# Keys and queries loaded as rows of two positions on 96 partitions instead of eight on 72

## The chip, the cores and the metric

The kernel runs on one core of a Trainium2 chip. Its time is the device time of one execution in microseconds, the median over several runs.

## The reference

Three layers in a row, all in float32:

```python
# attention: q, k, v of 4 batches, 8 heads, 576 positions, 64 dimensions
scores = scale * np.matmul(q, k.transpose(0, 1, 3, 2))
mask = (rel >= 0) & (rel < 64)               # rel = query position - key position
scores = np.where(mask, scores, -1000000000.0)
attn = np.exp(scores - np.max(scores, axis=-1, keepdims=True))
attn = attn / (np.sum(attn, axis=-1, keepdims=True) + 1e-09)
x = np.matmul(attn, v)                       # then 2304 tokens of 512
# one expert of eight for each token, by the largest of xn @ en.T / tau
h = np.maximum(x[mask] @ w1[e], 0.0)
out[mask] = gate_w[mask, None] * (h @ w2[e])
# a layer for all tokens
r = np.maximum(x @ w_in, 0.0)
out = (s * (r * r) + b) @ w_out
```

## The kernel before

The work has three stages: attention with the choice of experts (up to about 200 us), the experts one after the other, and the last layers. The change lies in attention.

Attention works on 16 units, a unit being two heads (hp and hp + 4) of one batch, which lie on the two halves of the partitions. A unit has nine windows of 64 queries; a step takes three windows, so there are 48 steps. In a step TensorE multiplies the queries of a window of both heads (qbd, a block-diagonal tile) with 128 keys (kT) into sp (L250). VectorE adds the mask and takes the minimum (sm and mn, L255), GpSimd takes it off (L258), ScalarE exponentiates into pe (L265, L268), TensorE flips pe into pt (L274), ScalarE copies that to pT (L276), TensorE multiplies pT with the values vb into pob (L285), and VectorE divides into xs (L288 to L290). The PSUM tile pt has one buffer. Between the steps stand transposes of xs (tpx, copied to xt by ScalarE at L382) and the router's products and sums (rt). Most of a step's later operations run one or two steps behind its scores.

Keys and queries arrive with positions on partitions and have to be turned so that the 64 dimensions lie on partitions. load_qk (L159 to L165) loads the keys and the queries of a unit each with one DMA: partition p of 72 gets eight positions in a row, of both heads, 2 KB a head. prep (L217 to L242) turns a unit in four pieces (keys and queries, of two heads each). A piece is four transposes of [72, 128], each of two neighbouring positions (L227), into one PSUM tile tp of three buffers. The upper half of the partitions then holds the even positions, the lower half the odd ones, and two copies bring them to their places in kT or qbd:

```python
o = kT[rows].rearrange("r (p j e) -> r e j p", j=hj, e=2)[:, par]
i = pt[64 * par:64 * par + 64]
```

Neighbouring elements of i thus go to places eight elements (32 bytes) apart. Both copies of the keys, and the even one of the queries, are ScalarE's (L237); the odd one of the queries is VectorE's (L239).

TensorE's order and SyncE's order are the order of the code (manual_schedule). A rule (AHEAD, RATE) spreads the pieces of prep over the steps. The order on ScalarE, VectorE and GpSimd is made by a scheduler that estimates times. After the pieces of unit n stand, on SyncE's queue, the load of unit n + 2's keys and queries, which reuse the four raw buffers, and of unit n + 1's values (L193); between them stand the stores of xs to x_dram (L687). The tau that VectorE turns into itau (L353) comes on ScalarE's DMA queue.

Of the kernel before, what the change touches and what calls it, by code (L numbers as in the profile page):

```python
# [8 lines left out]
F32 = mybir.dt.float32  # L9
# [11 lines left out]
def tile_kernel(ctx, tc, q, k, v, emb, tau, w1, w2, w_in, w_out, s_in, b_in, out, x_dram, y_dram, y0_dram, wi_dram, wo_dram):  # L21
    nc = tc.nc
    B, H, S, D = q.shape
    NT, DM = out.shape
    NP = H // 2
    NW = S // 64
    QP = 72
    QJ = S // QP
    BIG = 3.0e38

    E, _, F = w1.shape
    NTT = NT // 128
    # columns of tokens for the experts, the first one fixed before the others, these by falling count;
    # the first one's first NA columns are fixed early: of TF tiles of tokens, some expert has as many
    TF = 13
    TL = 15
    NA = 208
# [10 lines left out]
    ident = const.tile([128, 128], F32, name="ident")  # L48
    make_identity(nc, ident)

    # token and gate of an expert's columns; the token of a column among all
# [3 lines left out]
    # by order of work: expert, first column  # L55
# [4 lines left out]
    # tiles that are left over: expert, first rank, first column, number  # L60
# [5 lines left out]
    # of a token: its expert (E less it), its rank there; its number and gate in parts  # L66
    km = const.tile([128, NTT], F32, name="km")
    rank = const.tile([128, NTT], F32, name="rank")
# [20 lines left out]
    def load_part(src, le=nc.vector):  # L89
        """a source of [128, 1024], then its high and low parts"""  # L90
        n = nchunk[0]
        nchunk[0] += 1
        ring = rings[0] if n % KR < 8 else rings[1]
        raw = raw_p.tile([128, 1024], F32, tag="raw", name="raw")
        nc.sync.dma_start(raw if len(src.shape) == 2 else raw.rearrange("p (r d) -> p r d", r=2), src)
        h = ring.tile([128, 1024], F32R, tag="wh", name="wh")
        l = ring.tile([128, 1040 if ring is wa else 1024], F32R, tag="wl", name="wl")[:, :1024]
        return (h, l), lambda: split(raw, h, l, le)
# [14 lines left out]
    def turn(pp, xg, xt, o, c0=0):  # L113
        """a tile of rows, transposed, as high and low parts: columns c0.. to o.."""
        r = xg.shape[0]
        tp = pp.tile([128, ND, 128], F32, tag="tp", name="tp")
        for c in range(ND):
            nc.tensor.transpose(tp[:, c, :r], xg[:, c * 128:(c + 1) * 128], ident[:r, :r])
        o1 = o + r - c0
        return split(tp[:, :, c0:r], xt[0][:, :, o:o1], xt[1][:, :, o:o1], nc.vector)  # L120

    def three(ps, a, b, first, last):
        """ps += a[0] b[0] + a[0] b[1] + a[1] b[0], of high and low parts"""
        for j, (x, y) in enumerate(((0, 0), (0, 1), (1, 0))):
            nc.tensor.matmul(ps, a[x], b[y], start=first and j == 0, stop=last and j == 2)  # L125

    def summed(ps, pairs):
        """the like over pairs of a and b, with the low parts of b last"""
        k = [(a[x], b[y]) for x, y in ((0, 0), (1, 0), (0, 1)) for a, b in pairs]
        for j, (x, y) in enumerate(k):  # L130
            nc.tensor.matmul(ps, x, y, start=j == 0, stop=j == len(k) - 1)  # L131
# [27 lines left out]
    def load_qk(b, hp):  # L159
        r = []  # L160
        for nm, src in (("k", k), ("q", q)):
            t = raw_p.tile([128, 1024], F32, tag="raw", name=nm)[:QP].rearrange("p (h d) -> p h d", h=2)
            nc.sync.dma_start(t, src[b].rearrange("(t f) (p j) d -> f p t (j d)", f=NP, p=QP)[hp])
            r.append(t)
        qk[b, hp] = r  # L165
# [5 lines left out]
    # of eight pairs of heads; keys and values in the place of the first weights  # L171
# [16 lines left out]
    def load_v(b, hp):  # L188
        # slots 0..3: blocks 2t | 2t+1 on the halves; 4..7: blocks 2t+1 | 2t+2
        for i in range(2):  # L190
            for h in range(2):
                src = v[b, hp + h * NP, 64 * i:64 * i + 512].rearrange("(w p) d -> p w d", p=128)
                nc.sync.dma_start(vbufs[(b * NP + hp) % NB][:, 4 * i:4 * i + 4, h, :D], src)  # L193
# [7 lines left out]
    # masks: [0] the window of keys i-1, i; [1] the first window, keys 0, 1  # L201
# [15 lines left out]
    def prep(b, hp):  # L217
        """transposes of a pair of heads, in four pieces"""
        kt, qt = qk.pop((b, hp))
        qd = qbd[(b * NP + hp) % NB]  # L220
        kT = kTs[(b * NP + hp) % NB]
        hj = QJ // 2
        for nm, src in (("k", kt), ("q", qt)):
            for h in range(2):
                pt = ps3.tile([128, hj, QP], F32, tag="tp", name="tp")
                for jj in range(hj):
                    nc.tensor.transpose(pt[:, jj], src[:, h, jj * 2 * D:(jj + 1) * 2 * D], ident[:QP, :QP])  # L227
                rows = slice(64 * h, 64 * h + 64)
                for par in range(2):
                    if nm == "k":  # L230
                        o = kT[rows].rearrange("r (p j e) -> r e j p", j=hj, e=2)[:, par]
                        i = pt[64 * par:64 * par + 64]
                    else:
                        o = qd[rows, :, h].rearrange("r w (p j e) -> r e j w p", j=hj, e=2)[:, par]
                        i = pt[64 * par:64 * par + 64].rearrange("r j (w p) -> r j w p", w=NW)
                    if par == 0 or (nm, h) in TOACT:
                        nc.scalar.activation(o, i, AF.Copy)  # L237
                    else:
                        nc.vector.tensor_copy(o, i)  # L239
                if nm == "q" and h == 1:  # L240
                    ready[b, hp] = qd, kT
                yield  # L242
# [91 lines left out]
    def router_setup():  # L334
# [20 lines left out]
        # everything in this bank adds up from zeros  # L355
# [53 lines left out]
    def block(kk, ln, a):  # L409
        """a = 128 kk + ln"""  # L410
        nc.vector.tensor_scalar(kk, a, 1.0 / 128.0, -127.0 / 256.0, op0=ALU.mult, op1=ALU.add)
        nc.vector.tensor_scalar(kk, kk, 12582912.0, -12582912.0, op0=ALU.add, op1=ALU.add)
        nc.vector.scalar_tensor_tensor(ln, kk, -128.0, a, op0=ALU.mult, op1=ALU.add)
# [22 lines left out]
    def route_list(t0, t1):  # L436
        n = t1 - t0
        ts_ = slice(t0, t1)
        # rank among the tokens of the same expert
# [3 lines left out]
        # its tile and its lane there  # L443
# [4 lines left out]
        # the experts' lists of tokens  # L448
# [24 lines left out]
    def route_gate(t0, t1):  # L473
        n = t1 - t0
        ts_ = slice(t0, t1)
        # gate: 1 / (sum exp(l - max) + 1e-9), as three bfloat16 parts that add up to it
# [19 lines left out]
    def route_first(t):  # L496
        """the expert with the most of the first t tiles' tokens"""
        u = rp.tile([128, E], F32, name="uf")
        nc.vector.scalar_tensor_tensor(u, R[:, t], W8, c7, op0=ALU.mult, op1=ALU.add)
        m = rp.tile([128, 1], F32, name="mf")  # L500
        nc.vector.tensor_reduce(m, u, axis=AX.X, op=ALU.max)
        nc.vector.tensor_scalar(ohf, u, m, None, op0=ALU.is_equal)
        ef = rp.tile([1, E], F32, name="ef")
        nc.vector.tensor_tensor(ef, ohf[0:1], iota[0:1, :E], op=ALU.mult)
        ff = rp.tile([1, 1], F32, name="ff")
        nc.vector.tensor_reduce(ff, ef, axis=AX.X, op=ALU.add)
        nc.vector.tensor_copy(efi, ff)
# [8 lines left out]
    def first_list(j0, j1, v0, v1):  # L516
        """values of columns j0..j1 of the first expert's list"""
# [18 lines left out]
    def route_order():  # L536
# [13 lines left out]
        # first column of an expert  # L550
# [13 lines left out]
    def by_order(dst, src, og):  # L564
        """an expert's list, by order of work"""
# [22 lines left out]
    def route_rest(cnt, og, oc):  # L588
        # the token of each column
# [32 lines left out]
        # tiles that the experts' columns don't hold, by expert  # L622
# [36 lines left out]
        # its first rank: the expert's columns and 128 for each tile before, or its last 128 tokens  # L659
# [127 lines left out]
    def first_part():  # L787
        """the first expert's first tokens, in twelve pieces"""
# [48 lines left out]
    # pieces of transposes by step: so many ahead of need, or a rate that stays below RATE  # L837
    AHEAD, RATE = 3, 1.9
    # in steps P0.. to PS the maximum is taken off on GpSimd, one step earlier than the exponentials need it
    P0, PS = 2, 42  # L840
    # pieces of the first expert's first tokens between the last steps
# [70 lines left out]
    def fetch(g):  # L912
        """an expert's tokens"""
# [9 lines left out]
    # between them, the choice of experts for the last tokens, and the rest of that expert's tokens  # L923
    with tc.manual_schedule(engines={mybir.EngineType.PE}):
# [20 lines left out]
        # columns from NA on  # L945
# [57 lines left out]
    def f64_part(n, rp=None):  # L1003
        """32 blocks of [128, 512] of the two weights, from float64 bits to float32, one half before the other"""
# [11 lines left out]
        # the high word's sign, exponent and 20 bits, as a float32  # L1016
        nc.vector.tensor_scalar(t, hi, 3, 0x3fffffff, op0=ALU.logical_shift_left, op1=ALU.bitwise_and)
        nc.vector.scalar_tensor_tensor(t, hi, -(1 << 30), t, op0=ALU.bitwise_and, op1=ALU.bitwise_or)
        # the low word's 32 bits, times that sign and exponent
# [9 lines left out]
    def overflow(mo):  # L1029
        """the tiles of tokens that an expert's own columns don't hold, one at a time"""  # L1030
# [262 lines left out]
```

## Time and profile before

| | |
|---|---|
| median of 3 runs | 855.96 us (855.43 to 857.25) |
| span of the profiled execution | 855.3 us |
| busy share of the span | PE 94%, PEld 87%, DVE 62%, ACT 49%, POOL 29% |
| mean granted TensorE clock | 0.978 |
| DMA packets | 88705, 117.14 MB |

The profile gives the span of the execution from its first to its last instruction and no other time for it. PE is TensorE's matmuls, PEld its weight loads, DVE VectorE, ACT ScalarE, POOL GpSimd, SP SyncE; a q behind the name is the engine's queue. A matmul in float32 shows as two records, a transpose as one. The last column of a timeline row is the idle time of the engine ahead of it and what ended it.

### The profile page before, as it was taken

Reading aid. Unit: us, or ns where it says so; the run is one execution under the profiler, and the core shown is the slowest. Engines: PE = TensorE matmul, PEld = TensorE weight load, DVE = VectorE, ACT = ScalarE, POOL = GpSimd, SP = SyncE. Lnnn points to the kernel's source line nnn. Section 1 sums busy time; section 2 is a strip of 40 time slices with the busy share of each in tenths; the row PEclk is TensorE's granted clock in tenths of the full one; section 3 lists DMA queues with packets and bytes.
Section 4 is the critical chain, followed back from the end, with each engine's and each line's share of the span. In section 5 each row is a group of like instructions: output and inputs, shape, how many; then the busy total and the mean of one; then the engine's idle time right before and its main releaser. Section 6 shows DMA issues by size and latency. Waiting matters only on the chain. (4 is left out here: it accounts for less than half of the span.)

```text
span 855.3 us, 16295 instructions
## 1 busy us (share of the span) xinstructions
PE 806.6 (94%) x6142; PEld 743.9 (87%) x6142; DVE 532.3 (62%) x1358; ACT 415.5 (49%) x813; POOL 251.1 (29%) x281
## 2 busy tenths in 40 slices
PE   5989988689999999989899999999999999999997
PEld 4868777579999999979899999999999999998885
DVE  4567798777787786879765555566655444444442
ACT  6798786541534545445354444444545333233331
POOL 6156764543201514524402222222210110111110
PEclk9799999889999999999989999999999999999999
DMA  8787763715666877788275222233332211100000
GB/s 178 150 194 147 156 130 74 225 33 180 216 198 233 285 246 237 250 268 287 105 246 175 86 97 99 99 117 112 114 114 79 72 50 50 50 26 25 25 25 25
DMA packets 88705, 117.14 MB, mean 137 GB/s; under 512 B 38468, under 2 KB 57924, under 8 KB 88624
## 3 DMA queue, kind: packets, MB, share of 16 engines
q1 hardware_dynamic: 79136, 99.11, 39.7%
q0 software_dynamic: 3232, 10.24, 3.3%
q10 hardware_dynamic: 6256, 6.72, 2.4%
q8 instruction: 49, 0.80, 0.4%
q14 instruction: 32, 0.26, 0.1%
HBM read 91.52 MB, written 24.53 MB: 136 GB/s over the span
## 5 line engine op out<-in xcount | busy, mean ns | idle before, releaser
L125 PE MATMUL p<-xl,wh 128*128 128x256 f32 x576 | 162.4, 282 | 0.0
L125 PE MATMUL p<-xh,wh 128*128 128x256 f32 x576 | 162.2, 282 | 0.0
L125 PE MATMUL p<-xh,wl 128*128 128x256 f32 x576 | 161.7, 281 | 0.0
L1200 ACT ACTIVATE r<-p 128x256 f32<-128x256 f32 x144 | 55.3, 384 | 167.8 <-PE p L125 164.7
L1201 DVE SCALAR_TENSOR_TENSOR r<-r,s_bc 128x256 f32<-128x256 f32 x144 | 80.9, 564 | 81.4 <-ACT r L1200 81.3
L1024 POOL TENSOR_TENSOR fl<-fl,fs 128x512 f32<-128x512 f32 x32 | 45.8, 1433 | 251.6 <-DVE fs L1023 226.7
L125 PE MATMUL p<-wh,gh 128*128 128x512 f32 x288 | 113.0, 392 | 0.0
L125 PE MATMUL p<-wl,gh 128*128 128x512 f32 x288 | 113.0, 392 | 0.0
L125 PE MATMUL p<-wh,gl 128*128 128x512 f32 x288 | 113.0, 392 | 0.0
L125 PEld LDWEIGHTS p<-xh,wh 128*128 128x128 f32 x576 | 108.8, 189 | 0.7
L125 PEld LDWEIGHTS p<-xl,wh 128*128 128x128 f32 x576 | 108.6, 189 | 0.8
L125 PEld LDWEIGHTS p<-xh,wl 128*128 128x128 f32 x576 | 109.0, 189 | 0.0
L87 DVE TENSOR_TENSOR wl<-raw,wh 128x1024 fp32r<-128x1024 f32 x72 | 101.9, 1423 | 7.0 <-ACT wh L86 6.7
L86 ACT ACTIVATE wh<-raw 128x1024 fp32r<-128x1024 f32 x80 | 83.2, 1056 | 6.6 <-DMA raw<-wo_dram 3.4
L125 PE MATMUL p<-hh,wh 128*128 128x256 f32 (+5 forms) x256 | 78.7, 307 | 0.0
L1239 POOL DMA_INDIRECT out_dram<-o,ids x18 | 19.1, 1061 | 202.9 <-DVE o L1238 181.5
L125 PE MATMUL p<-hl,wh 128*128 128x256 f32 (+5 forms) x256 | 77.0, 301 | 0.0
L125 PE MATMUL p<-hh,wl 128*128 128x256 f32 (+5 forms) x256 | 76.9, 300 | 0.0
L1207 ACT ACTIVATE gh<-r,b_bc 128x256 fp32r<-128x256 f32 x144 | 72.4, 503 | 8.6 <-DVE r L1201 8.6
L1208 DVE SCALAR_TENSOR_TENSOR gl<-r,b_bc,gh 128x256 fp32r<-128x256 f32 x144 | 69.0, 479 | 3.1 <-ACT gh L1207 3.1
L125 PEld LDWEIGHTS p<-wh,gl 128*128 128x128 f32 x288 | 54.1, 188 | 12.1
L125 PEld LDWEIGHTS p<-wh,gh 128*128 128x128 f32 x288 | 54.1, 188 | 11.4
(240 smaller groups left out, 1635.8 us busy)
## 6 DMA issues: line engine op xcount, KB each, us to landing
raw<-in_moe_w_dram SPq DMA_DIRECT2D x64, 512.0 KB
raw<-y_dram SPq DMA_DIRECT2D x18, 512.0 KB
vb<-in_v_dram SPq DMA_DIRECT2D x64, 128.0 KB
fr<-in_moe_w_in_dram SPq DMA_DIRECT2D x16, 512.0 KB
fr<-in_moe_w_out_dram SPq DMA_DIRECT2D x16, 512.0 KB
k<-in_k_dram SPq DMA_DIRECT2D x16, 288.0 KB
q<-in_q_dram SPq DMA_DIRECT2D x16, 288.0 KB
x_dram<-xs SPq DMA_DIRECT2D x24, 192.0 KB
```

Of the source, the lines that this page charges most:

```text
L86: a = nc.scalar.activation(hi, src, AF.Copy)
L87: return a.ins, le.tensor_tensor(lo, src, hi.bitcast(F32), op=ALU.subtract).ins
L125: nc.tensor.matmul(ps, a[x], b[y], start=first and j == 0, stop=last and j == 2)
L1024: nc.gpsimd.tensor_tensor(lf, lf, sg.bitcast(F32), op=ALU.mult)
L1200: nc.scalar.activation(r, ps, AF.Relu)
L1201: nc.vector.scalar_tensor_tensor(r, r, s_bc, r, op0=ALU.mult, op1=ALU.mult)
L1207: nc.scalar.activation(gh, r, AF.Identity, bias=b_bc)
L1208: nc.vector.scalar_tensor_tensor(gl, r, b_bc, gh.bitcast(F32), op0=ALU.add, op1=ALU.subtract)
L1239: nc.gpsimd.indirect_dma_start(out=out, out_offset=bass.IndirectOffsetOnAxis(ap=ids[:, k:k + 1], axis=0), in_=o, in_offset=None)
```

## The change

Partition p of 96 now gets two positions in a row, three times (c), 192 positions apart; a piece is three transposes of [96, 128]. Each head has its own DMA, in pieces of 512 bytes. Neighbouring elements of a transposed block now go to places two elements (8 bytes) apart. All comments of the file were taken out too.

```diff
-    QP = 72
-    QJ = S // QP
+    QP = 96
+    QC = S // (2 * QP)
...
-            t = raw_p.tile([128, 1024], F32, tag="raw", name=nm)[:QP].rearrange("p (h d) -> p h d", h=2)
-            nc.sync.dma_start(t, src[b].rearrange("(t f) (p j) d -> f p t (j d)", f=NP, p=QP)[hp])
+            t = raw_p.tile([128, 1024], F32, tag="raw", name=nm)[:QP, :2 * QC * 128].rearrange("p (h c d) -> p h c d", h=2, c=QC)
+            for h in range(2):
+                nc.sync.dma_start(t[:, h], src[b, hp + h * NP].rearrange("(c p e) d -> p c (e d)", c=QC, e=2))
...
-        hj = QJ // 2
...
-                pt = ps3.tile([128, hj, QP], F32, tag="tp", name="tp")
-                for jj in range(hj):
-                    nc.tensor.transpose(pt[:, jj], src[:, h, jj * 2 * D:(jj + 1) * 2 * D], ident[:QP, :QP])
+                pt = ps3.tile([128, QC, QP], F32, tag="tp", name="tp")
+                for c in range(QC):
+                    nc.tensor.transpose(pt[:, c], src[:, h, c], ident[:QP, :QP])
...
-                        o = kT[rows].rearrange("r (p j e) -> r e j p", j=hj, e=2)[:, par]
+                        o = kT[rows].rearrange("r (c p e) -> r e c p", c=QC, e=2)[:, par]
...
-                        o = qd[rows, :, h].rearrange("r w (p j e) -> r e j w p", j=hj, e=2)[:, par]
-                        i = pt[64 * par:64 * par + 64].rearrange("r j (w p) -> r j w p", w=NW)
+                        o = qd[rows, :, h].rearrange("r (c w) (p e) -> r e c w p", c=QC, e=2)[:, par]
+                        i = pt[64 * par:64 * par + 64].rearrange("r c (w p) -> r c w p", p=32)
```

Line numbers of the changed file are one or two higher from here on. TensorE's order has the same rows, with six transposes of 96 columns where eight of 72 stood. On VectorE, at the start: iota and pid are the router's small tables, w, c and val follow from them, qbd are the queries' copies of the first unit. Before:

```order
L353 RECIPROCAL itau<-tau_bc 128x1
L336 CAST iota<-iota_i 128x128
L239 COPY qbd_133<-tp 64x4x9x8
L338 CAST pid<-pid_i 128x1
L339 TENSOR_SCALAR w_191<-iota 128x8
L239 COPY qbd_133<-tp 64x4x9x8
L340 TENSOR_SCALAR c_192<-iota 128x8
L344 CAST val<-iota 128x18
L343 CAST val<-pid 128x18
L255 ISA sm,mn<-sp,mask 128x128
```

And in the changed kernel:

```order
L354 RECIPROCAL itau<-tau_bc 128x1
L337 CAST iota<-iota_i 128x128
L339 CAST pid<-pid_i 128x1
L240 COPY qbd_135<-tp 64x9x32
L340 TENSOR_SCALAR w_195<-iota 128x8
L341 TENSOR_SCALAR c_196<-iota 128x8
L344 CAST val<-pid 128x18
L345 CAST val<-iota 128x18
L240 COPY qbd_135<-tp 64x9x32
L256 ISA sm,mn<-sp,mask 128x128
```

The second copy of the queries now stands behind w, c and val; pid stands ahead of the first. On ScalarE at the start, before (kT and qbd are the copies, pe the exponentials, pT the flipped ones):

```order
L237 ACTIVATE qbd_133<-tp 64x4x9x8 x2
L357 DMA em<-in_moe_expert_emb_dram 8x512
L237 ACTIVATE kT<-tp 64x4x72 x4
L268 ACTIVATE pe<-sm,mn 128x128
L237 ACTIVATE qbd_134<-tp 64x4x9x8
L268 ACTIVATE pe<-sm,mn 128x128 x2
L237 ACTIVATE qbd_134<-tp 64x4x9x8
L268 ACTIVATE pe<-sm,mn 128x128
L237 ACTIVATE kT<-tp 64x4x72 x2
L268 ACTIVATE pe<-sm,mn 128x128 x2
L237 ACTIVATE kT<-tp 64x4x72 x2
L276 ACTIVATE pT<-pt 128x384 x2
```

And in the changed kernel:

```order
L358 DMA em<-in_moe_expert_emb_dram 8x512
L238 ACTIVATE qbd_135<-tp 64x9x32
L238 ACTIVATE kT<-tp 64x288 x4
L269 ACTIVATE pe<-sm,mn 128x128
L238 ACTIVATE qbd_136<-tp 64x9x32
L269 ACTIVATE pe<-sm,mn 128x128 x2
L238 ACTIVATE qbd_136<-tp 64x9x32
L238 ACTIVATE kT<-tp 64x288 x2
L269 ACTIVATE pe<-sm,mn 128x128
L238 ACTIVATE kT<-tp 64x288 x2
L269 ACTIVATE pe<-sm,mn 128x128 x2
L277 ACTIVATE pT<-pt 128x384
```

From the first scores to the first pT the same exponentials and copies stand, two of the keys' copies an exponential earlier. On SyncE's queue, the loads ahead of the first steps, before:

```order
L163 DMA k<-in_k_dram 72x2x512
L163 DMA q<-in_q_dram 72x2x512
L163 DMA k<-in_k_dram 72x2x512
L163 DMA q<-in_q_dram 72x2x512
L193 DMA vb<-in_v_dram 128x4x64 x4
```

And in the changed kernel:

```order
L165 DMA k<-in_k_dram 96x3x128 x2
L165 DMA q<-in_q_dram 96x3x128 x2
L165 DMA k<-in_k_dram 96x3x128 x2
L165 DMA q<-in_q_dram 96x3x128 x2
L195 DMA vb<-in_v_dram 128x4x64 x4
```

Each DMA of keys or queries has become two, in the same places among the loads of values.

## Rows read from the trace of the kernel before

**Rows 1.** The page's first part: busy us and share by engine.
```profile
PE 806.6 (94%) x6142; PEld 743.9 (87%) x6142; DVE 532.3 (62%) x1358; ACT 415.5 (49%) x813; POOL 251.1 (29%) x281
```
**Rows 2.** Stages: us, busy PE, PEld, DVE, ACT, POOL (count), clock, DMA share, GB/s.
```profile
0.00:23.00 23.00, 12.86 (x93) 11.22 (x94) 10.54 (x49) 15.97 (x28) 14.30 (x49) 1.00 0.89 182
23.00:33.00 10.00, 10.00 (x67) 8.24 (x65) 5.33 (x25) 6.72 (x12) 1.65 (x2) 0.50 0.56 120
33.00:134.00 101.00, 91.09 (x1119) 77.46 (x1119) 73.20 (x351) 85.88 (x161) 62.41 (x103) 1.00 0.76 157
134.00:163.00 29.00, 21.96 (x277) 18.19 (x277) 25.10 (x135) 17.49 (x45) 18.76 (x17) 1.00 0.42 134
```
**Rows 3.** Groups by shape, the turned copies: busy us, mean ns, idle before.
```profile
L237 ACT ACTIVATE kT<-tp 64x288 f32<-64x288 f32 x64 | 44.2, 691 | 7.2 <-PE tp L227 6.4
L239 DVE COPY qbd<-tp 64x288 f32<-64x288 f32 x32 | 22.0, 689 | 15.1 <-ACT qbd L237 14.5
L237 ACT ACTIVATE qbd<-tp 64x288 f32<-64x288 f32 x32 | 22.0, 688 | 3.4 <-PE tp L227 2.9
```
**Rows 4.** Groups by shape, whole span: other copies of like size.
```profile
L1021 ACT ACTIVATE fl<-fr 128x512 f32<-128x512 uint32 x32 | 21.2, 667 | 43.5 <-POOL ft L1026 41.1 <-DMA fr<-in_moe_w_out_dram 2.0 <-DMA fr<-in_moe_w_in_dram 0.4
L86 ACT ACTIVATE xh<-tp 128x512 fp32r<-128x512 f32 x17 | 10.2, 599 | 27.4 <-PE tp L118 27.3
...
L781 ACT ACTIVATE y<-p 128x296 f32<-128x296 f32 x2 | 0.8, 419 | 3.8 <-PE p L125 3.8
L779 DVE COPY y<-p 128x296 f32<-128x296 f32 x2 | 0.8, 456 | 0.0
```
**Rows 5.** Waits of weight loads, 33 to 134 us: us, times, longest.
```profile
PEld pt L274 <- ACT pT L276: 3.6, 5, 1.0
PEld pob L285 <- DVE xs L290: 3.1, 5, 1.0
...
PEld tpx L380 <- DVE xs L290: 2.0, 3, 1.3
PEld tp L227 <- ACT xt L382: 1.0, 1, 1.0
PEld tpx L380 <- DVE qbd L239: 0.8, 1, 0.8
PEld tp L227 <- DVE qbd L239: 0.8, 3, 0.4
```
**Rows 6.** Timeline of the start: start us, us, instruction, idle before.
```profile
9.16 0.16 DVE L353 RECIPROCAL itau<-tau_bc 128x1 f32<-128x1 f32 x1 [6.63 <-DMA tau_bc<-in_moe_tau_dram]
...
10.79 0.68 DVE L239 COPY qbd<-tp 64x288 f32<-64x288 f32 x1
...
11.52 1.36 PEld L250 LDWEIGHTS sp<-kT,qbd 128*128 128x128 f32 x6 [0.23 <-DVE qbd L239]
...
20.49 0.49 ACT L276 ACTIVATE pT<-pt 128x384 f32<-128x384 f32 x1
21.04 0.31 PEld L274 LDWEIGHTS pt<-ident,pe 128*128 128x128 f32 x3 [2.85 <-ACT pT L276]
```
**Rows 7.** Timeline later: three flips, and eight transposes.
```profile
104.96 0.36 PEld L274 LDWEIGHTS pt<-ident,pe 128*128 128x128 f32 x3
...
110.12 0.58 PEld L227 LDWEIGHTS tp<-ident,q 72*128 72x128 f32 x8
```
**Rows 8.** DMA in 9.75:11.25, 52:53, 4.5:6 (packets, MB, share); packets in 33:134.
```profile
q1 hardware_dynamic: 1026, 0.25, 101.0%
...
q1 hardware_dynamic: 153, 0.16, 67.7%
...
q1 hardware_dynamic: 184, 0.35, 72.6%
...
DMA packets 31964, 15.84 MB, mean 157 GB/s; under 512 B 25852, under 2 KB 28924, under 8 KB 31948
```
**Rows 9.** Waits of SyncE's queue, 0 to 134 us.
```profile
SPq L163 <- PE tp L227: 20.7, 10, 6.5
```

## Prediction

> **What bounds the kernel now.** I read the busy time by stage first. Up to 134 us ScalarE (ACT) and TensorE (PE) are both nearly full: from 33 to 134 us, 101 us long, PE is busy 91.09 us, its weight loads (PEld) 77.46, ACT 85.88, VectorE (DVE) 73.20, and the DMA engines 0.76 [rows 2]. The transposes of keys and queries that the change touches all lie before 134 us; the 29 us after them hold attention and routing without any (PE 21.96) [rows 2]. In the page's first line PE is busy 94% of the whole span [rows 1], so from the routing on, work that starts earlier ends earlier.
>
> Then the groups by shape: ACT spends 44.2 us on 64 copies of keys and 22.0 us on 32 of queries, DVE 22.0 us on 32 of queries, each 688 to 691 ns for 64x288 [rows 3]. Both engines copy 296 contiguous elements a partition from PSUM in 419 and 456 ns [rows 4]. So a copy of 288 written in steps of 32 bytes takes some 270 ns (ACT) and 240 ns (DVE) longer than a packed one would.
>
> Last, what PE waits for. From 33 to 134 us the weight loads waited for ACT 3.6 us (pT, before the flips) and 1.0 us (xt), 0.8 + 0.8 us for the DVE copy of queries, and 3.1 + 2.0 us for DVE's xs [rows 5]: 4.6 us by ACT, 1.6 by the copies on DVE, 5.1 by other DVE work. That is the whole room in that stretch; the rest of PE is work. SyncE's queue waited 20.7 us for transposes to free a raw buffer before the next key or query load [rows 9]: the loads are ahead of their use, and DMA does not set the pace.
>
> **The change, part by part.** *Transposes.* Of 256 transposes with 72 columns, 192 with 96 are left; both make 288 columns for a head's keys or queries. Eight of 72 columns take 0.58 us of weight loads, three flips of 128 columns 0.36 us [rows 7]: 72.5 and 120 ns each, so 0.85 ns a column and 11 ns fixed. At 96 columns that makes 93 ns, and six make 0.56 us against 0.58. Saved: 32 x 0.02 = 0.6 us over the stage, which I count as nothing. PE gets no shorter work, although it gets a quarter fewer instructions.
>
> *Copies.* Their number and size stay (96 on ACT, 32 on DVE); only the step of the write falls from 32 to 8 bytes. No row shows an 8-byte write. Bounds: as packed, 412 ns on ACT and 449 on DVE (the 296-element rows less 8 elements), or no gain, 691 and 689. The nearest row reads 512 elements in 8-byte steps on ACT: 667 ns, against 599 for packed ones [rows 4]; 68 ns in 512 is 0.13 ns an element, 38 ns in 288. I take 450 ns on ACT and 487 on DVE. ACT then saves 96 x 0.241 = 23.1 us (bounds 0 to 26.8), DVE 32 x 0.202 = 6.5 us (0 to 7.7). Most of that lies beside PE's work, so it isn't the gain.
>
> The row says that a 32-byte step costs two thirds more than none. The Trainium skill, "SBUF — State Buffer", section "Door 1: The DMA port swizzle", says that SBUF is accessed in lines of 16 bytes and that a step of up to four fp32 elements is free as long as a line is hit at least twice. By that the new copies would stand at the packed bound, and the sum below would be some 0.3 us better; the trace agrees for the old step and shows nothing of the new.
>
> *What of the copies stands on the path: the start.* The first scores run at 11.52 us, when DVE's second copy of queries (10.79, 0.68 us) is done; DVE's queue stood until 9.16 us for tau's DMA [rows 6]. Six ACT copies ahead of it get 0.24 us shorter, but DVE still waits for tau, and its order now puts the small preparations between its two copies of queries, not behind them. From 9.16: reciprocal, iota and pid to 9.7, a copy to 10.2, four small operations some 0.6 us, a copy to 11.3. So the first scores come 0.25 us earlier, no more (bounds: 1.2 us if tau lands sooner, -0.4 if later). From there to the second pT ACT runs, in order, exponentials and six copies (two of queries, four of keys), and PE stands 2.85 us for that pT [rows 6]. From the first scores to pT it takes 20.49 - 11.52 = 8.97 us. With six copies shorter by 0.24 (1.45 us) and a DVE copy of 0.2 in the middle, plus the 0.5 us by which ACT's wait for the second step's maximum shrinks, it takes 6.9. Start: 0.25 + 2.1 = 2.4 us.
>
> *The middle.* Each ACT-caused wait of PE is 0.7 to 1.0 us, with two to four copies queued ahead, worth 0.5 to 1.0 us. I let 4.0 of the 4.6 us go, 1.0 of the 1.6 us of query copies, and none of the 5.1 us for xs, where DVE's routing operations stand ahead. What is late next is PE itself and then xs. Middle: 5.0 us (bounds 0 to 11.3, all waits of [rows 5]).
>
> *Loads.* Four issues of 144 KB for a pair of heads, not two of 288 KB, and 512-byte pieces, not 2 KB. On SyncE that is 32 more issues, some 0.4 us each, in a queue that waits 20.7 us anyway. What queues behind them are the value loads and the stores of x_dram. Price of a packet, from the share of 16 engines: 256 bytes 1.01 x 16 x 1.5 / 1026 = 24 ns; 1 KB 0.677 x 16 x 1.0 / 153 = 71 ns; 2 KB 0.726 x 16 x 1.5 / 184 = 95 ns [rows 8]. For 512 bytes the bounds are 24 and 71; on the line between them by bytes, 40 ns. From 33 to 134 us there are 31948 - 28924 = 3024 packets of 2 KB or more [rows 8], some 18 us of 16 engines; 12096 of 512 bytes take 30.2 us. The share rises from 76 to 88 us of 101: covered, at no cost. Bounds: 18 us (no change) to 54 us.
>
> *Sum* against the profiled span of 855.3 us: 2.4 + 5.0 = 7.4, so 847.9. The profile has no second clock for its execution; the median of the runs, 855.96, is 0.66 us above the span. 847.9 + 0.66 = 848.6; I predict 848.5.
>
> **The rivals.** *A. More than the waits: the clock.* From 23 to 33 us PE ran at granted 0.50 (1.2 GHz) with no idle time (10.00 of 10.00), behind its 2.85 us stand; before and after that the row is at 1.00 (2.4 GHz) [rows 2, 6]. If a shorter stand lets the clock stay up, 8.24 us of weight loads are worth 4.1 less at most; with that and two of the xs waits, 848.6 - 6 = 842.5. For it: the drop follows the stand at once. Against: the start itself stays slow, and a stand of about 1 us remains.
>
> *B. The gain sinks into DVE and POOL.* PE's order interleaves chains through DVE (xs waits 5.1 us) and POOL; ACT freed of 23 us just waits for them. Then only the start counts: 855.96 - 2.4 = 853.5. For it: DVE is busy 25.10 of 29 us at the end of attention. Against: between 33 and 134 us DVE has 28 us free.
>
> *C. The copies don't get faster*, as an 8-byte step may cost what a 32-byte one does: only order moves, 856, within 1 us. For it: no row of a write at that step. Against: ACT and DVE read at that step nearly as fast as packed [rows 4].
>
> *D. Slower: the loads become the bound.* If a 512-byte packet takes what one of 1 KB takes, 71 ns, then 12096 x 71 / 16 = 54 us stand where 18 did, 36 more than now, and the free share is 24.7 us. PE waits the other 11 us for keys and values: 855.96 + 11 - 2.4 = 864.5. It decides from 57 ns a packet on (12096 x 57 / 16 - 18 = 25). Against: 256 bytes take 24 ns, under load too.
>
> **How the numbers follow.** The forecast has 0.50, with its own range 845 to 852; A 0.16, B 0.14, C 0.11, D 0.09. A measurement of this kernel tells 0.2% (1.7 us) from no change. Faster is the forecast, A and most of B: 0.79. Same is C and a little of B: 0.12; slower is D: 0.09. For eight in ten I leave out D and the far half of A: 841.5 to 855.5.
>
> **What would show it.** Right: copies of 64x288 near 450 ns on ACT; the second pT near 18 us; PE's waits for pT and xt from 33 to 134 us gone or under 1 us; six transposes in about 0.56 us; the last transposes near 126 us, not 133. Wrong: copies still near 690 ns (C); PE's weight loads waiting for k, q or vb (D); PE's waits for xs grown by what pT's fell (B). A half-clock stretch that isn't there before 33 us speaks for A.

## The result, and the profile after

The changed kernel takes 840.25 us (median of 4 runs, 838.74 to 842.60) against 855.69 us for the kernel before beside it (4 runs, 855.09 to 857.25). The ratio is 0.983, its 95% interval 0.981 to 0.985. The gain is 15.4 us where 7.5 were forecast (855.96 to 848.5), and the time lies below the predicted range.

The profiled execution has a span of 837.0 us, 18.3 less than before. That pair makes the gain look larger than the medians do: the profiled run after is the quickest of its four, and the one before was one of the slower ones (the runs on record stand 1.7 to 1.8 us above their own spans, so a span of 855.3 goes with some 857). The span is used for where the time went, the medians for how much.

The page's first part answers to [rows 1], and its row of the granted clock follows (40 slices of the span, tenths of full speed):

```profile
PE 800.7 (96%) x6078; PEld 741.3 (89%) x6078; DVE 525.3 (63%) x1358; ACT 391.8 (47%) x813; POOL 250.2 (30%) x281
...
PEclk9999998889999999999999999999999999999999
```

PE has 64 transposes fewer (6142 to 6078). ACT fell by 23.7 us, DVE by 7.0, and PE, with no other instruction taken from it, by 5.9. The groups by shape answer to [rows 3]:

```profile
L238 ACT ACTIVATE kT<-tp 64x288 f32<-64x288 f32 x64 | 27.4, 428 | 6.5 <-PE tp L228 5.8
L240 DVE COPY qbd<-tp 64x288 f32<-64x288 f32 x32 | 14.7, 460 | 6.4 <-ACT qbd L238 5.7
L238 ACT ACTIVATE qbd<-tp 64x288 f32<-64x288 f32 x32 | 13.6, 424 | 2.1 <-PE tp L228 1.6
```

Each copy is 230 to 265 ns shorter. The second thing to see is in DVE's line: its idle time behind ACT's even copy of the queries was 14.5 us [rows 3] and is 5.7.

The stages answer to [rows 2], with the same columns. The same work now ends some 20 us sooner, so the cuts lie elsewhere:

```profile
0.00:18.00 18.00, 12.63 (x77) 10.92 (x78) 9.12 (x46) 11.78 (x28) 14.29 (x48) 1.00 1.03 198
18.00:25.00 7.00, 6.97 (x83) 5.73 (x82) 5.46 (x29) 5.50 (x13) 1.72 (x3) 1.00 1.23 212
25.00:113.00 88.00, 85.92 (x1053) 74.80 (x1052) 67.47 (x353) 67.70 (x160) 62.37 (x103) 1.00 0.82 184
113.00:143.00 30.00, 23.42 (x283) 19.93 (x280) 24.30 (x133) 17.58 (x44) 18.70 (x18) 0.94 0.42 129
```

Before, 10 us behind the start ran at granted 0.50 [rows 2]; here the clock is 1.00 up to 113 us. In the long stage PE is idle 2.1 us of 88, where it was idle 9.9 us of 101. The weight loads' waits there, answering to [rows 5]:

```profile
PEld tpx L381 <- DVE xs L291: 2.0, 3, 1.1
...
PEld pob L286 <- DVE xs L291: 0.4, 2, 0.2
```

None for pT, xt or the queries' copies is left, and those for xs fell from 5.1 to 2.4 us. The start, answering to [rows 6]:

```profile
4.18 0.93 PEld L228 LDWEIGHTS tp<-ident,k 96*128 96x128 f32 x6 [4.18 <-POOL qbd L181]
...
5.62 0.16 DVE L354 RECIPROCAL itau<-tau_bc 128x1 f32<-128x1 f32 x1 [3.09 <-DMA tau_bc<-in_moe_tau_dram]
...
8.32 0.46 DVE L240 COPY qbd<-tp 64x288 f32<-64x288 f32 x1
8.84 1.35 PEld L251 LDWEIGHTS sp<-kT,qbd 128*128 128x128 f32 x6 [0.68 <-DVE qbd L240]
...
16.06 0.49 ACT L277 ACTIVATE pT<-pt 128x384 f32<-128x384 f32 x1
16.60 0.31 PEld L275 LDWEIGHTS pt<-ident,pe 128*128 128x128 f32 x3 [0.72 <-ACT pT L277]
17.58 0.53 PEld L228 LDWEIGHTS tp<-ident,q 96*128 96x128 f32 x6
```

Keys, tau and the first scores are all early, and PE's stand for pT is 0.72 us, not 2.85. (The row of the first transposes names POOL, but POOL had done with that qbd at 3.87; the keys' DMA came later.) Where the lead comes from is read by following the same events through both timelines (starts of PE's matmuls):

| us into the span | before | after | lead |
|---|---|---|---|
| first scores | 11.52 | 8.84 | 2.7 |
| scores of the 5th step | 22.57 | 18.13 | 4.4 |
| scores of the 8th step | 33.93 | 25.10 | 8.8 |
| last transposes of keys or queries | 130.85 | 110.37 | 20.5 |
| last scores and products of attention | 170.35 | 149.86 | 20.5 |
| first expert starts | 195.92 | 174.65 | 21.3 |
| 30 us later | | | 18.4 |
| end | 855.3 | 837.0 | 18.3 |

So the start gives 4.4 us, the stretch in which the clock had been low 4.4, the middle 11.7, and some 2.9 are lost again at the first expert.

### The profile page after: what moved, and what is told of

It reads as the page before. It is cut to its first block, busy times and chain, and to the rows that moved or that the text cites. A ratio compares the mean times of both kernels' runs of the same rounds, so it can differ in the third digit from the quotient of the medians.

```text
span 837.0 us, 16214 instructions
## 1 busy us (share of the span) xinstructions
PE 800.7 (96%) x6078; PEld 741.3 (89%) x6078; DVE 525.3 (63%) x1358; ACT 391.8 (47%) x813; POOL 250.2 (30%) x281
## 4 chain that ended last, share of the span: by engine, by line
PE 50%; issue 0%; DMA 0%; POOLq 0%; DVE 0%
PE p L126 49%; PE tp L132 1%; DMA out_dram<-o,ids 0%; POOLq L1289 0%; DVE o L1239 0%; POOLq L1240 0%
```

## The experiments

The theory: the shorter copies do it all, as ACT and DVE get out of PE's way, and the rest follows from that. The rivals: the loads (split by head, in other pieces), or the clock. Times of the middle are those from the 8th step's scores to the last transposes: 96.9 us before, 85.3 after. Four more executions of the changed kernel's attention in that stretch (below: a longer stand at the start, pieces of 1536 bytes, the changed kernel once more, later gatings) took 85.3 us each, so half a microsecond counts there even in a single profile.

**Only the step of the write undone.** Loads and transposes of the changed kernel, all 128 copies in 32-byte steps; the positions come out in another order, so the output is other.

```diff
-o = kT[rows].rearrange("r (c p e) -> r e c p", c=QC, e=2)[:, par]
+o = kT[rows].rearrange("r (p j e) -> r e j p", j=4, e=2)[:, par]
...
-o = qd[rows, :, h].rearrange("r (c w) (p e) -> r e c w p", c=QC, e=2)[:, par]
+o = qd[rows, :, h].rearrange("r w (p j e) -> r e j w p", j=4, e=2)[:, par]
```

> The changed kernel's loads and transposes, but all copies write in 32-byte steps as before (keys and queries come to the wrong places, so the output is another; the work in attention is the same). Theory (the step makes all but the earlier landing of the first loads): copies at 690 ns again; the first scores near 9.5 to 10 us, because the keys still land at 4.2; TensorE's stand before the second flip over 2 us and the clock at half again behind it; from there to the last transposes waits for pT of 3 to 5 us again; the first scores' lead over the kernel before (1.5 to 2 us) stays about the same to the end of attention, where the changed kernel had 20. Rival (the loads make a good part of the gain): the lead at the end of attention is 8 us or more.

Measured: 854.3 us in one run, span 852.6; as the output is other, the stages behind attention get other data. The copies take 686 to 692 ns, the middle 96.2 us, and the old waits are back (weight loads, 30 to 126 us):

```profile
PEld pt L275 <- ACT pT L277: 3.0, 4, 1.1
...
PEld pob L286 <- DVE xs L291: 2.7, 5, 1.0
PEld tpx L381 <- DVE xs L291: 2.5, 3, 1.3
PEld tp L228 <- DVE qbd L240: 1.8, 4, 0.9
PEld tp L228 <- ACT xt L383: 1.1, 1, 1.1
```

So the step makes the middle. But at the end of attention this kernel still leads the one before by 6.1 us: keys at 4.17, tau at 5.49, first scores at 10.3, and no low clock at the start, behind a stand of 1.55 us:

```profile
10.29 1.35 PEld L251 LDWEIGHTS sp<-kT,qbd 128*128 128x128 f32 x6 [0.65 <-DVE qbd L240]
...
19.00 0.31 PEld L275 LDWEIGHTS pt<-ident,pe 128*128 128x128 f32 x3 [1.55 <-ACT pT L277]
```

The theory had a lead of 1.5 to 2 us and the half clock back; it missed both. The loads do more than it gave them.

**The other way round: only the step changed.** The kernel before, with its loads as they are, and copies in 8-byte steps (output other). The text on record says that the loads are split; they were not.

```diff
-o = kT[rows].rearrange("r (p j e) -> r e j p", j=hj, e=2)[:, par]
+o = kT[rows].rearrange("r (j p e) -> r e j p", j=hj, e=2)[:, par]
```

> The same split loads of 2 KB on 72 partitions, with all copies written in 8-byte steps (keys and queries come to the wrong places, the output is another; the work in attention is the same). Theory (split and write step are the whole change): copies of 424 to 460 ns, the stretch from the eighth step's scores to the last transposes 85 to 88 us as in the changed kernel (97 before), a lead of 17 to 20 us at the end of attention. Rival (512-byte pieces on 96 partitions add something of their own): a lead under 14.

Its whole time, 876.55 us, says nothing, since the later stages get other data. In attention: copies of 426 to 461 ns, middle 86.0 us, no low clock, and a lead of 16.3 us at the end of attention (154.07). Keys and tau land late as before (6.08, 10.22). The step alone gives four fifths of the lead; the loads add what lies between 16.3 and 20.5. The loads alone gave 6.1 (the experiment before). That makes 22.4 with the step's 16.3, more than both together: each of the two had no low clock at the start, and that counts twice. Up to the 5th step it is the other way round: the loads alone lead by 2.0 us there, the step alone by 1.0, both together by 4.4.

**72 partitions.** The changed kernel with four transposes of 72 columns a piece (and the queries' places in the copy to match):

```diff
-    QP = 96
+    QP = 72
```

> The changed kernel with 72 partitions in place of 96: rows of two positions (512 bytes), one DMA a head, four transposes of 72 columns a piece, the write still in 8-byte steps. Theory (the write's step makes the gain, the 96 partitions do nothing): copies of 64x288 at 424 to 460 ns, first scores within 0.5 us of 8.84 us, no half clock before 30 us, time within 2 us of the changed kernel's 840. Rival (96 partitions matter, by spreading the loads over more of the DMA engines or by fewer transposes): the first keys land 1 us or more later than 4.2 us, waits of TensorE for keys, queries or values appear, and the time is 845 or more.

Measured: 842.21 us (839.23 to 845.04, 4 runs), ratio 0.984 [0.979, 0.990]. The middle takes 87.8 us; around 37 to 44 us the transposes wait for keys, which they never do on 96 partitions:

```profile
37.31 0.33 PEld L228 LDWEIGHTS tp<-ident,k 72*128 72x128 f32 x4 [0.26 <-DMA k<-in_k_dram]
...
43.87 0.44 PE L228 MATMUL tp<-ident,k 72*128 72x72 f32 x4 [0.37 <-DMA k<-in_k_dram]
```

In these two profiles the 96 partitions are worth 4.1 us at the end of attention (153.92 against 149.86). The whole times don't tell the two apart.

**Pieces of 1536 bytes.** Each partition gets six positions in a row (output other), so that a head's load has one piece a partition, not three of 512 bytes.

```diff
-"(c p e) d -> p c (e d)"
+"(p c e) d -> p c (e d)"
```

> The changed kernel with the loads as rows of six positions (1536-byte pieces) on the same 96 partitions, one DMA a head; copies unchanged, so keys and queries come to the wrong places and the output is another. Tells what of the load made the first keys land at 4.2 us instead of 5.7 and tau at 5.6 instead of 9.2. If it is the short pieces: keys near 5 to 5.5 us, tau near 8, first scores 1 us or more later than 8.84. If it is the halved DMAs or the 96 partitions: within 0.3 us of the changed kernel. The middle of attention should be the same in both cases.

Measured: 836.41 us in one run (its later stages get other data); keys at 3.80, tau 5.38, first scores 8.27, middle 85.3. Short pieces don't make the early landing: with longer ones the keys come 0.4 us and the first scores 0.6 us earlier still. The middle is the same with either.

**Only the loads split.** The kernel before, with one DMA a head (2 KB pieces, 72 partitions):

```diff
-nc.sync.dma_start(t, src[b].rearrange("(t f) (p j) d -> f p t (j d)", f=NP, p=QP)[hp])
+for h in range(2):
+    nc.sync.dma_start(t[:, h], src[b, hp + h * NP].rearrange("(p j) d -> p (j d)", p=QP))
```

> The kernel before, with each load of keys or queries split into one DMA a head (2 KB pieces, 72 partitions, 32-byte writes all as before). Theory (the keys of the changed kernel land earlier because the first head's DMA is half as long, not because of the partitions or the pieces): first transposes at 4.3 to 4.6 us, tau before 7 us, first scores near 10.3 us, a lead of 4 to 6 us at the end of attention with the half clock at 23 us gone or shorter, time 850 to 853. Rival (the spread over 96 partitions or the short pieces make it): first transposes at 5.5 us or later, nothing else moves, 855.

Measured: 856.08 us (10 runs, 851.60 to 865.00) against 855.94 (13 runs, 852.45 to 863.21); the ratio, without the run of 865.00, is 1.000 [0.996, 1.004]. The profiled run took 857.35. Its start:

```profile
3.86 0.53 PEld L228 LDWEIGHTS tp<-ident,k 72*128 72x128 f32 x4 [3.86 <-POOL qbd L179]
...
4.89 0.53 PEld L228 LDWEIGHTS tp<-ident,k 72*128 72x128 f32 x4 [0.50 <-DMA k<-in_k_dram]
...
6.57 0.16 DVE L354 RECIPROCAL itau<-tau_bc 128x1 f32<-128x1 f32 x1 [4.04 <-DMA tau_bc<-in_moe_tau_dram]
...
10.33 1.36 PEld L251 LDWEIGHTS sp<-kT,qbd 128*128 128x128 f32 x6 [0.90 <-DVE qbd L240]
```

The split alone brings the keys 1.8 us and tau 2.6 us forward, and the first scores 1.2: the first head's transposes begin before the second head's keys are there, and the second head's wait 0.5 us for those. It led by 5.3 us at the 8th step (28.68) and by 0.5 us at the end of attention. Stages of it:

```profile
29.00:53.70 24.70, 20.01 (x242) 16.75 (x242) 16.59 (x86) 23.34 (x42) 11.02 (x17) 1.00 0.80 188
53.70:63.90 10.20, 10.20 (x65) 8.71 (x66) 3.37 (x16) 6.25 (x13) 4.27 (x8) 0.50 0.84 206
```

With the slow copies PE stands 4.7 us of the 24.7, and then the clock falls to 0.50 (1.2 GHz) for 10.2 us, here at 53.7 instead of 23 us. The early landing is real, and in this profile little of it was left at the end of attention, because a low clock came later; the 850 to 853 us that were expected did not come in the median either. Why the low clock came there is open: the first experiment, with the same slow copies, had none up to the end of its transposes.

**A longer stand at the start.** The changed kernel, the first pT copied six times:

```diff
+for _ in range(6 if len(pts) == 0 else 1):
     nc.scalar.activation(pT, pt, AF.Copy)
```

> The changed kernel, with the first pT copied six times in a row instead of once, so that TensorE stands some 2.5 to 3 us before the second flip as it did before the change. Theory (the stand brought the half clock, its absence is worth 4.4 us): a stretch at half clock from about 20 to 30 us, and the scores of the eighth step 6 to 7 us later than in the changed kernel (2.4 the copies, 4 the clock). Rival (the clock follows something else of the start): no such stretch, 2.5 us later and no more.

Measured: 842.90 us (841.02 to 843.74, 4 runs), ratio 0.986 [0.981, 0.990]. The stand, and the two stretches behind it (columns as in the stages):

```profile
19.45 0.50 PEld L275 LDWEIGHTS pt<-ident,pe 128*128 128x128 f32 x3 [4.62 <-ACT pT L278]
```

```profile
20.00:30.00 10.00, 10.00 (x74) 8.09 (x72) 4.00 (x21) 4.37 (x10) 0.99 (x2) 0.52 0.61 141
30.00:40.00 10.00, 10.00 (x121) 8.82 (x121) 8.08 (x46) 8.19 (x20) 3.95 (x7) 1.00 0.57 135
```

The clock falls behind the stand, as it does in the kernel before. From the 5th step to the 8th it takes 10.03 us against 6.97: 3.1 us are the clock's. Here the low clock begins before the 5th step, too: from the flip behind the stand to the scores of that step the same instructions take 2.71 us against 1.52. So the clock costs 4.2 us in all; the other 2.8 are the flip's, which starts that much later behind the stand. The 7.1 us that it lost by the 8th step shrank to 2.3 in the spans (839.3 against 837.0): lead at the start is partly given back later.

**Which copies.** Three kernels, each the changed one with part of its copies in 32-byte steps (outputs other): the 64 of keys on ACT; the 64 of queries (32 on ACT, 32 on DVE); the 32 of queries on DVE alone. The edits are those of the first experiment, for the keys or for the queries alone; the third has it under `if par == 1`.

> The changed kernel with the copies of keys alone, all on ScalarE, written in 32-byte steps (output another). ScalarE gets back 64 x 0.264 = 17 us, VectorE nothing. Theory (TensorE waits for ScalarE's queue, and VectorE's lateness follows from it): the stretch from the eighth step's scores to the last transposes grows from 85.3 to some 92 us, waits for pT come back, waits for xs partly. Rival (VectorE's copies decide): under 88 us.

> The changed kernel with the copies of queries alone written in 32-byte steps (output another): ScalarE gets back 32 x 0.264 = 8.5 us, VectorE 32 x 0.23 = 7.3 us. Theory (ScalarE's load decides): the stretch from the eighth step's scores to the last transposes grows by half of what slow keys cost, to some 88 us. Rival (VectorE's copies decide): it grows more than with slow keys, to 92 us or beyond, with waits for xs and for the queries' copies.

> The changed kernel with only the odd copies of queries, the 32 on VectorE, written in 32-byte steps (output another): VectorE gets back 7.3 us, ScalarE nothing. With all queries slow the stretch from the eighth step's scores to the last transposes was 90.0 us, with keys slow 92.0, in the changed kernel 85.3. Theory (ScalarE's load makes the stretch, VectorE's lateness follows from standing behind ScalarE's even copy): 85.3 to 86.5 us. Rival (VectorE's own time counts as much): 87.5 us or more, with waits for xs.

| slow copies | middle, us | over 85.3 | weight loads' waits there: pT + xt, xs, query copies | whole, one run (later stages get other data) |
|---|---|---|---|---|
| keys (ACT, 17.0 us more) | 92.0 | 6.7 | 5.1, 2.5, 0.8 | 921.43 |
| queries (ACT 8.4, DVE 7.3) | 90.0 | 4.8 | 0, 4.5, 1.9 | 844.74 |
| queries on DVE (7.3) | 88.3 | 3.0 | 0, 4.1, 0.9 | 841.82 |

The keys came out as expected, the queries between theory and rival, and the third kernel as its rival had it. Keys and queries nearly add up: 6.7 + 4.8 = 11.5, where both slow together gave 10.9 (96.2 in the first experiment). Of the queries' 4.8, DVE's own time makes 3.0 and ACT's even copies, behind which DVE stands, the other 1.8. So the waits for xs are also the copies' doing: DVE divides into xs from one queue with its copies of the queries and its stands for ACT's. This is DVE's group in the long stage after, and in the kernel before (33 to 134 us):

```profile
L240 DVE COPY qbd<-tp 64x288 f32<-64x288 f32 x25 | 11.5, 461 | 3.6 <-ACT qbd L238 3.0
```

```profile
L239 DVE COPY qbd<-tp 64x288 f32<-64x288 f32 x25 | 17.3, 691 | 12.3 <-ACT qbd L237 11.7
```

DVE got back 5.8 us of work and 8.7 us of standing there.

**What is given back, and a better version.** At the first expert PE turns tiles of gathered tokens; each is then split into a high part xh (by ACT) and a low part xl (by DVE), which go into the products. In the changed kernel PE stands at the last of these tiles:

```profile
188.03 0.48 DVE L112 TENSOR_SCALAR xg<-xg,gsl 128x512 f32<-128x512 f32 x1 [1.66 <-DMA xg<-x_dram,idx]
...
190.38 0.49 DVE L112 TENSOR_SCALAR xg<-xg,gsl 128x512 f32<-128x512 f32 x1 [1.58 <-DMA xg<-x_dram,idx]
...
191.32 0.53 PEld L132 LDWEIGHTS tp<-xl,wh 128*128 128x128 f32 x4 [2.76 <-DVE xl L88]
...
192.93 0.97 PEld L132 LDWEIGHTS tp<-xl,wh 128*128 128x128 f32 x4
```

DVE's queue has the second expert's gatings (L112, the gathered tokens xg times their gates gsl), which wait for their gathers, ahead of the low part that PE needs. The same wait in the kernel before:

```profile
211.23 0.53 PEld L131 LDWEIGHTS tp<-xl,wh 128*128 128x128 f32 x4 [1.11 <-DVE xl L87]
```

After the longer one four weight loads take 0.97 us, not 0.53: the low clock again, 3.4 us long (columns as in the stages):

```profile
192.40:195.80 3.40, 3.40 (x19) 3.40 (x18) 1.45 (x4) 1.41 (x3) 0.00 (x0) 0.51 0.38 107
```

Two kernels against it: one that places the second expert's gatings behind that low part, and one that also gives the odd queries of a unit's second head to ACT.

```diff
-    def fetch(g):
+    def fetch(g, after=()):
...
-            gated(xg, gsl[:r, g, j:j + 1])
+            with ExitStack() as st:
+                for a in after:
+                    st.enter_context(tc.issue_after(a))
+                gated(xg, gsl[:r, g, j:j + 1])
...
-            turn(ps3, xg, x0, o, c0)
+            turned0 = turn(ps3, xg, x0, o, c0)
...
-                xgs[:] = fetch(n + 1)
+                xgs[:] = fetch(n + 1, turned0[1:] if n == 0 else ())
```

```diff
-    TOACT = (("k", 0), ("k", 1))
+    TOACT = (("k", 0), ("k", 1), ("q", 1))
```

> The changed kernel itself, on the chip of the two variants beside it, so that these are compared with it and not only with the kernel before. Every theory: 838 to 843 us, half-clock stretches behind attention at varying places.

> The changed kernel, with VectorE's gating of the second expert's gathered tokens placed behind the low part of the first expert's last turned tile. In the changed kernel VectorE stands 1.6 us twice for gathers there, and TensorE 2.8 us behind it, with a half-clock stretch after that. Theory (2.9 us of the gain were given back there): TensorE's stand before the first expert's remaining tokens under 1 us, the lead at the first expert 21 us and not 18, 2 to 4 us faster than the changed kernel. Rival (the gathers are then late for the second expert, or the clock falls elsewhere): no difference that shows.

> The variant with the turned tile first, and in attention also the odd copy of the second head's queries moved from VectorE to ScalarE (16 of 32). ScalarE gets 6.8 us more, VectorE 7.4 less. Theory (with fast copies ScalarE has room and the rest of TensorE's waits, 2.4 us for xs, is VectorE's): the stretch from the eighth step's scores to the last transposes 84 us, first scores 0.5 us earlier, another 1 us faster. Rival (ScalarE is still the tighter of the two): the stretch grows to 87 us, waits for pT come back.

Measured on one chip, 5 runs each, the kernel before at 854.71: the changed kernel 837.48 (836.67 to 838.50), ratio 0.980 [0.978, 0.981]; with the gatings later 833.43 (831.53 to 835.01), ratio 0.974 [0.972, 0.977]; with the queries on ACT too 833.43 (832.17 to 835.35), ratio 0.975 [0.973, 0.977]. With the later gatings the stand is gone:

```profile
188.05 0.54 PEld L132 LDWEIGHTS tp<-xh,wh 128*128 128x128 f32 x4 [0.68 <-ACT xh L87]
...
188.99 0.54 PEld L132 LDWEIGHTS tp<-xl,wh 128*128 128x128 f32 x4
```

Some 4 us, the best version of this study. Moving queries to ACT gains nothing: the middle grows from 85.3 to 86.4 us, near the rival's 87, as the waits for xs shrink from 2.2 to 2.1 us only, and 1.0 for pT and 0.9 for xt come back.

## Why the prediction was wrong in size, step by step

**Transposes: right.** Six take 0.53 us where 0.56 were forecast.

**Copies: right.** 424 to 428 and 460 ns, against 450 and 487. ACT saved 25.2 us by its groups, where 23.1 were forecast, DVE 7.3 for 6.5. They stand 11 to 16 ns above the packed bound of the prediction, and so near what the rule of the Trainium skill named there ("SBUF — State Buffer", "Door 1: The DMA port swizzle") makes of them. Rival C is out. Its argument against named DVE as well; the rows it pointed to hold such a read for ACT alone.

**Start: the failed step is "DVE still waits for tau" until 9.16 us.** It took the landings as fixed; -0.4 to 1.2 us were its bounds. Keys came 1.5 us and tau 3.5 us earlier, and the first scores 2.7, not 0.25. The cause of the landings is in the change but not in its copies: one DMA a head. Only the loads split gives 1.8 and 2.6 us, longer pieces land a little earlier still, and with the loads whole both land late. Most of the rest of tau's 3.5 us comes with the 96 partitions (6.24 on 72, 5.62 on 96). The first scores take both parts of the change: with the early landing and slow copies they come at 10.3, 1.2 us earlier, with quick copies and the late landing at 11.92; the other 1.5 us are the copies', once tau no longer holds DVE up. Why tau, from another queue, is early as well is not settled; that it stood behind less is only a guess. The other term, from the first scores to the second pT, was nearly right: the lead grew by 1.8 us (2.7 to 4.4 at the 5th step; 1.4 with the step alone), where 2.1 were forecast.

**Clock: the sum took it as unchanged, and left a change of it to rival A.** It was 10 us at 0.50 before and none after; from the 5th to the 8th step that is 4.4 us. By the kernel with only the writes undone (8.04 us against 11.36 before, both with slow copies) the clock's part is 3.3, and the other 1.1 (8.04 to 6.97) the copies'; the stand put back at the start gives 3.1 for these steps. Rival A had "4.1 less at most". Its argument against, "a stand of about 1 us remains", was true (0.72) and didn't count.

**Middle: 11.7 us, where 5.0 were forecast and 11.3 was the bound.** PE's own idle time by what ended it, in that stretch (33.93 to 130.85 us before, 25.10 to 110.37 after), shows which parts failed:

```profile
PE pob L285 <- DVE xs L290: 2.9, 4, 0.9
PE pt L274 <- ACT pT L276: 2.6, 4, 0.8
PE tpx L380 <- DVE xs L290: 1.4, 2, 1.1
PE pob L285 <- issue: 0.9, 2, 0.7
PE tp L227 <- ACT xt L382: 0.9, 1, 0.9
PE tpx L380 <- DVE qbd L239: 0.6, 1, 0.6
PE tp L227 <- DVE qbd L239: 0.3, 1, 0.3
```

```profile
PE tpx L381 <- DVE xs L291: 1.3, 2, 0.8
PE pob L286 <- DVE xs L291: 0.3, 1, 0.3
PE pob L286 <- DVE km L428: 0.3, 1, 0.3
```

ACT's waits gave 3.5 us (forecast 4.0), the queries' copies 0.9 (1.0): right. Two sentences were wrong. "None of the 5.1 us for xs, where DVE's routing operations stand ahead": 2.7 us went, by these rows and by [rows 5] alike. The row that says why was in the prediction's own rows, DVE's 14.5 us behind ACT's copies [rows 3], and it read only the busy column of it. And "the rest of PE is work": in the same stretch, with the same steps, PE's busy time fell too. Busy times are the second number of each line, for the kernel before, the one with only the step changed, and after:

```profile
33.93:130.85 96.92, 87.01 (x1069) 74.00 (x1068) 70.65 (x339) 82.29 (x153) 60.77 (x101) 1.00 0.78 161
```

```profile
28.61:114.58 85.97, 83.86 (x1070) 73.13 (x1068) 65.83 (x342) 65.61 (x155) 61.50 (x101) 1.00 0.89 184
```

```profile
25.10:110.37 85.27, 83.19 (x1021) 72.49 (x1019) 65.35 (x342) 65.54 (x155) 61.18 (x101) 1.00 0.83 187
```

From 87.0 to 83.9 us no instruction of PE changed, only the copies' step: 3.1 us that the records call busy went with the waits. Most likely records overlap less around a wait, but no run shows that by itself. The last 0.7 comes with the rest of the edit, the transposes of 96 columns and the loads (0.6 was worked out for the transposes, "which I count as nothing"); the transposes' own busy time there hardly differs (17.8 us with only the step changed, 17.7 after). The sum: idle 9.9 - 2.1 = 7.8, busy 3.8, together 11.6.

**Loads: right, they cost nothing, but closer than it looked.** On 96 partitions no transpose in the long stage waits for keys or queries; in the changed kernel on 72 some do. The added DMA time was put too high: 88 us of 101 were forecast, and 0.82 of 88 us is 72, less than the 77 before (0.76 of 101).

**Rivals.** B is refuted: PE's waits for xs fell. D is not seen. A was the nearest (842.5 us, with two of the xs waits) and still 2 us short, as it had no early landing. Of the signs, the second pT came at 16.06 (18 was forecast) and the last transposes at 110.37 (126 was forecast; before they stood at 130.85, not at 133). The step from the span to the time, 0.66 us, was also too small: 1.7 to 1.8 us on record. The sum as it should have been, by the spans: 4.4 + 4.4 + 11.7 + 0.8 up to the first expert - 2.9 there = 18.4, against 18.3.

## What to carry to other kernels

A copy's step can be worth far more than the copy where it stands in two in-order queues: follow the idle column of the engine that waits for the copy, not only its busy one, and ask which of its later operations the critical engine needs. Where PE waits often, its gain can exceed the sum of its waits in the profile, so leave the upper bound open. Look at every part of an edit for what it brings forward too (here a load split in two; at the start it and the copies gave more together than each by itself), and look for the next stand once work starts earlier: a queue in which other work waits for DMA ahead of the needed instruction took back 3 of 21 us, and reordering it gave 4.

## What the runs showed of the hardware that was not expected

- A write of 64x288 from PSUM takes 428 ns on ACT and 460 on DVE in 8-byte steps, 691 and 689 in 32-byte steps.
- A 288 KB load split into two of 144 KB let the first half be used 1.8 us sooner, and a small load on another queue landed 2.6 us sooner.
- Behind stands of 2.85 and 4.62 us at the start the granted clock was 0.50 to 0.52 for about 10 us; behind stands of 0.72 and 1.55 us it stayed at 1.00. The kernel before with its loads split, behind a stretch with PE idle 4.7 of 24.7 us, had 0.50 for 10.2 us from 53.7 us on.
